# The product with v in 64 by 64 cells from a dense tile, apart from the scores

## The chip, the cores and the metric

One core of a Trainium2 chip runs the whole kernel. The metric is the device time of the program in microseconds, the median of several runs. The engines are named as the profile names them: PE is TensorE (matmuls; PEld its weight loads), DVE is VectorE, ACT is ScalarE, POOL is GpSimd, SP issues DMAs.

## The reference

Attention over chunks of 32 queries with a short window and 8 memory keys, followed by a two-layer network with a squared ReLU. Four batches, 8 heads, 768 tokens, head size 64; the network is 512 by 2048 by 512 on 3072 tokens.

```python
chunk, left_ctx, right_ctx = (32, 16, 8); n_mem = 8
for c in range(nc):                       # 24 chunks of a sequence
    k_full = concat([mem_k, k[l_start:r_end]]); v_full = concat([mem_v, v[l_start:r_end]])
    scores = scale * q_c @ k_full.T
    a = exp(scores - max(scores)); a = a / (sum(a) + 1e-09)
    out[c_start:c_end] = a @ v_full
x = out.transpose(0, 2, 1, 3).reshape(B * S, H * D)
h = x @ w_in
g = s * maximum(h, 0) ** 2 + b
return g @ w_out
```

Each chunk sees 16 + 32 + 8 context keys and 8 memory keys, a cell of 64 keys (`CELL`).

## The kernel before

Everything that the engines do is first listed as operations (`op`, line 208) with an engine, a held time from the table `HOLD` (line 134), a due time (`prio`) and the parts of tiles that they read and write. `Plan.lay` (line 229) plays that list through on a model of five engines and fixes the order of each; the program is then written out in that order. On each engine the instructions run in the order so found. An operation takes the earliest due among those that are ready; a due time is in steps, 40 for the first part and 3.75 for each of the 22 units of the second. Lists such as `VISITS`, `FLIPS`, `MIX`, `XSUM` hold due times, and `MIXENG`, `XENG`, `XENG1` choose VectorE or GpSimd for operations that either can do.

The tokens go in 8 groups of 384 (`ch`, two per batch). Attention of one group is made in two *visits* (`attend(ch, d)`), each with two pairs of heads. Groups 0 and 1 are made early. The later visits, 12 in all (groups 2 to 7), lie spread among the matmuls of the network, which fill TensorE otherwise: `hidden` (line 847) and `result` (line 870) for the groups 0 to 3, then units (`unit`, line 1041; `second`, line 1095) that make two groups of a batch together with seven products instead of eight.

A later visit goes so. `product` (line 667) makes the scores, 24 matmuls for each pair of heads, with 64 rows (the head size), 32 stationary columns (queries) and 64 moving columns (keys). VectorE and ScalarE make the softmax. `flip` (line 627) turns blocks of 32 by 32 on VectorE and sends them with eight DMAs into the tile `aT`, so that keys lie along the partitions. There two chunks of 64 keys are stacked, in a block-diagonal form: a chunk's 64 rows stand beside zeros in the columns of the other chunk. `value2` (line 684) makes the product with v from it, 24 matmuls with 128 rows, 64 stationary columns (v) and 64 moving columns (two chunks of 32 queries), into two PSUM banks, the first for 512 columns and the second for 256. All matmuls of the attention are in fp32, and each shows in the trace as two instructions with a weight load each. The network's matmuls are in the float32r form with high and low halves, which is why each result is split by ScalarE (`xhigh`, or `park` for the later groups) and VectorE (`xlow`).

For `aT` of the later visits there is one place (`diag`, line 452), the same memory that the two tiles of the early visits have. The values of a visit are made when the next visit begins: lines 786 to 795 put `value1`, `value2`, `scores1` and `scores2` in one chain, which TensorE runs without anything between, and which takes four PSUM banks (`S` and `V`, two each) at one time. Only the last visit's values stand alone (`last_[3]`, line 1198).

In `sums` (line 913) and `sums_of_parts` (line 948) sums and differences of the parked values are made, 768 columns each, and `mix` (line 982) does the like with weights.

Of the kernel before, what the change touches and what calls it, by code (L numbers as in the profile page):

```python
# [15 lines left out]
AF = mybir.ActivationFunctionType  # L16
# [61 lines left out]
POOLED = set()  # L78
MIX = [24.4, 26.07, 28.76, 31.57, 35.54, 36.93, 32.73, 30.93]
MIXENG = ['DVE', 'DVE', 'POOL', 'DVE', 'POOL', 'DVE', 'DVE', 'DVE']  # L80
XENG = ['POOL', 'POOL', 'DVE', 'POOL']
RELEASE = 22
AHEAD = -0.81
FLIPS = [3.49, 8.13, 6.86, 5.1, 9.6, 5.37, 4.05, -0.05, -0.86, 9.11, -1.0, -2.32]
PROD = [-0.08, 0.96, 0.26, 1.59, 3.42, 3.01, 3.43]
CHAIN = {'11': 1.68, '22': 0.22, '12': 4.42, '21': 6.47}
SECONDS = [6.99, 8.34, 6.63, 10.26]
XSUM = [1.29, -2.52, 0.98, -0.03]
XENG1 = ['DVE', 'POOL', 'POOL', 'POOL', 'DVE', 'DVE', 'POOL', 'DVE', 'DVE', 'POOL']
XSUM1 = [2.5, -0.8, 2.75, 1.29, 0.06, -0.47, 0.2, -3.8, 9.08, -7.14]  # L90
XSPLIT1 = [-5.65, -14.64, -0.76, -1.78]
XSPLIT = [-3.43, -3.64, 1.94, -0.12, 2.77, 4.93, 0.47]
RBANKS = 2
# [25 lines left out]
UNIT = 3.75  # L119
VISITS = [17.38, 22.0, 24.84, 30.0, 32.33, 43.05, 47.62, 56.46, 54.35, 67.42, 76.83, 76.57, 88.7]  # L120

# [6 lines left out]
for _u, (_, _f) in enumerate(STEPS):  # L128
# [4 lines left out]

HOLD = dict(hidden=523, result=690, half=365, first=850, scores=650, value1=1000, value2=530, scores1=500, scores2=600, turn=110, value=515, wrest=800, warm=215,
            relu=390, square=390, affine=565, high=388, xhigh=388, xhigh0=480, xhigh1=300, wscale=560, whigh=525, copy=270, exp6=480, exp3=340, keep=390, keepv=470, store=480,
            low=540, rec=90, edge=20, max6=490, max3=280, sub6=500, sub3=300, sum6=560, sum3=310, flip=580, xlow=470, xlow0=640, xlow1=400, wlow=350, wjoin=620, wsign=610, wdiff=610, out=600,
            small=235, part=290, wide=1040, tiny=200, norm6=1000, norm3=650, mul6=470, mul3=270, issue=440,
            prod=1036, result2=1362, save=482, hadd=554, hsq=553, hrelu=488, hsquare=517, haffine=706, hhigh=525, hlow=580,
            park0=589, park1=376, pre=1880, prev=936, khigh=840, klow=1000, accum=689, outcopy=597,
            mix2=1450, mix1=1000, mix2v=680, mix1v=410, thigh=623, tlow=675)  # L140
# [3 lines left out]
RATE, LAND, NEAR, FAR = 408.0, 2150.0, 6, 3400.0  # L144
CODE = dict(prod=12, result2=12, hidden=6, result=6, half=6, first=96, scores=96, value1=64, value2=32, scores1=96, scores2=96, turn=2, value=32)
BLOCK, SKEW = 256, 69
# [231 lines left out]
def body(ctx: ExitStack, tc: tile.TileContext, qkv, w1, w2, out):  # L378
# [72 lines left out]
    diags = Ring([wide_[:, n] for n in range(2)])  # L451
    diag = Ring([wide_])
    stats = Ring(stat_tiles)
# [185 lines left out]

    def attend(ch, d):  # L640
# [43 lines left out]
        def value2(m, V):  # L684
            for m6 in (2 * m, 2 * m + 1):
                for cp in range(2):
                    for n in range(2):
                        at = (((m6 % GB) * 2 + cp) * 2 + n) * D
                        to = V[m // 2].tile.rearrange("k (m r c q) -> k m r c q", r=2, c=2, q=CHUNK)[n * D:(n + 1) * D, m6 % 4, :, cp, :]
                        nc.tensor.matmul(to, vals_[m6 // GB].tile[:, at:at + D], aT[0].tile[:, n, :, cp * 2 * GB + m6, :], start=True, stop=True)  # L690

        def value(m, V):
# [3 lines left out]
            for c in range(NQC):  # L696
                for n in range(2):
                    half, at = divmod(((m * NQC + c) * 2 + n) * D, VW)
                    to = V[m // 2].tile.rearrange("k (m r c q) -> k m r c q", r=2, c=NQC, q=CHUNK)[n * D:(n + 1) * D, m % 2, :, c, :]
                    nc.tensor.matmul(to, vals_[half].tile[:, at:at + D], aT[n].tile[:, :, m * NQC + c, :], start=True, stop=True)  # L700

        def store(V):
            if ch >= 4:
                i = 2 * (ch % HALVES) + d
                for r in range(2):
                    lo, hi = (0, 4 * QB) if r == 0 else (4 * QB, 6 * QB)
                    firsts.append((ch // HALVES, 8, op("ACT", f"park{r}", due - 4, lambda lo=lo, hi=hi, r=r: nc.scalar.activation(park(i)[:, lo:hi], V[r].tile[:, :hi - lo], AF.Copy),
                       list(V[r].parts.values()), (c_park[i][r],))))
                if i == 3:
                    sums(ch // HALVES)  # L710
                return
            at = due + 0.9 if alone else due - 4
            for r in range(2):
                lo, hi = (0, 4 * QB) if r == 0 else (4 * QB, 6 * QB)
                to = lambda a, lo=lo, hi=hi: x.tile[:, (2 * a + d) * 2 * TOK + lo:(2 * a + d) * 2 * TOK + hi]
                fro = lambda r=r, lo=lo, hi=hi: V[r].tile[:, :hi - lo]
                got, kind = [z for z in V[r].parts.values()], str(r)
                op("ACT", "xhigh" + kind, at, lambda to=to, fro=fro: nc.scalar.activation(to(0), fro(), AF.Copy), got, (x["H", d, r],))
                op("DVE", "xlow" + kind, at, lambda to=to, fro=fro: nc.vector.tensor_tensor(to(1), fro(), to(0).bitcast(F32), ALU.subtract),
# [15 lines left out]
        def parts(V, at):  # L735
            return [op("PE", f"value{i + 1}", at, lambda ms=ms: [value(m, V) for m in ms], reads(ms), [V[i][0]]) for i, ms in enumerate(((0, 1), (2,)))]

        def soft(S):
            t, y = (None, None) if early else (Val(both), Val(diag))
            for n in range(2):  # L740
# [40 lines left out]
        else:  # L781
# [6 lines left out]
            for o in chain[1:]:  # L788
                for v in o.vals:
                    if v.ring is ps and v not in chain[0].vals:  # L790
                        chain[0].vals.append(v)
                        v.left += 1
            for o, nxt in zip(chain, chain[1:]):
                o.next = nxt
                if o not in nxt.deps:
                    nxt.deps.add(o)
            if last:
# [418 lines left out]
    for n in range(2):  # L1216
        hold(both, n, on(ts_))
    hold(diag, 0, on(diags))
    for n in range(7):
# [52 lines left out]
```

## Time and profile before

| | |
|---|---|
| median of 3 runs | 584.6 us (582.42 to 585.76) |
| profiled execution | 582.78 us, its span 581.0 us |
| TensorE busy | 571.2 us (98%) |
| VectorE, ScalarE, GpSimd busy | 381.0, 351.8, 58.0 us |
| bytes moved by DMA | 115.11 MB |

The span runs from the first to the last instruction of one profiled execution; some 2 us of the time lie around it. A line of a group gives the source line, engine, operation, output and input tiles, shape (partitions by elements; for matmuls first rows by columns of the stationary operand), the count, the busy time in us and the mean ns of one. In a timeline or a chain the first number is the start in us and the second the length.

### The profile page before, as it was taken

The numbers are of one execution on the slowest core, as the hardware profiler recorded it, in microseconds if no ns is written. First come the engines' busy times: TensorE is split into PE (matmuls) and PEld (weight loads), VectorE is DVE, ScalarE is ACT, GpSimd is POOL, SyncE is SP. The second block draws the span as 40 slices with busy tenths as digits, with TensorE's granted clock in tenths as the row PEclk, the third lists the DMA queues.
The fourth block names the chain that finished last, engine by engine and source line by source line (L and its number), as shares of the span: only waits on it lengthen the run. The fifth ranks groups of instructions, "written<-read, shape, count | busy, mean of one in ns | idle before, by whom it ended". The sixth has DMA issues, their size and how long they took to land.

```text
span 581.0 us, 12457 instructions
## 1 busy us (share of the span) xinstructions
PE 571.2 (98%) x4925; PEld 506.0 (87%) x4925; DVE 381.0 (66%) x796; ACT 351.8 (61%) x727; POOL 58.0 (10%) x59
## 2 busy tenths in 40 slices
PE   8989999999999999999999999999999999999997
PEld 4678998989889889899888899898999999999996
DVE  4988989988768988564769654565457434444442
ACT  6999888957657667454466454534466554444443
POOL 1000000001532241010131010011021000000000
PEclk9999999999999999999999999999999999999999
DMA  8995867843867978654674763745524543433002
GB/s 334 417 381 174 328 201 231 251 161 145 311 222 263 335 265 281 181 192 148 221 270 136 256 237 100 217 165 175 162 80 138 177 151 109 144 96 126 33 0 109
DMA packets 41882, 115.11 MB, mean 198 GB/s; under 512 B 5216, under 2 KB 13664, under 8 KB 41824
## 3 DMA queue, kind: packets, MB, share of 16 engines
q1 hardware_dynamic: 41824, 114.32, 57.4%
q8 instruction: 39, 0.64, 0.4%
q14 instruction: 19, 0.16, 0.1%
HBM read 88.61 MB, written 20.97 MB: 189 GB/s over the span
## 4 chain that ended last, share of the span: by engine, by line
PE 83%; DVE 6%; ACT 5%; DMA 4%; issue 1%; SPq 0%; ACTq 0%; DVEq 0%
PE ps L1053 27%; PE ps L1103 16%; PE ps L1133 16%; PE ps L879 9%; PE ps L855 9%; PE ps L690 3%; PE ps L675 3%; DMA words<-w 2%; DMA mixed<-words 1%; DMA early<-qkv 1%; ACT t L586 1%; DVE wv L837 1%; ACT ps L865 1%; DVE gL L867 1%; PE ps L700 1%
## 5 line engine op out<-in xcount | busy, mean ns | idle before, releaser
L1053 PE MATMUL ps<-x,ww 128*128 128x384 f32 x528 | 104.4, 336 | 0.0
L1072 ACT ACTIVATE gH<-words 128x384 fp32r<-128x384 f32 x66 | 34.6, 524 | 108.0 <-PE ps L1103 107.0
L1053 PEld LDWEIGHTS ps<-x,ww 128*128 128x128 f32 x528 | 93.8, 188 | 5.6
L1069 DVE TENSOR_TENSOR words<-ps,wv 128x384 f32<-128x384 f32 x66 | 34.9, 553 | 66.8 <-PE ps L1053 61.6
L1053 PE MATMUL ps<-home,ww 128*128 128x384 f32 x396 | 77.7, 338 | 0.0
L1053 PEld LDWEIGHTS ps<-home,ww 128*128 128x128 f32 x396 | 69.6, 188 | 2.9
L1150 DVE TENSOR_TENSOR partial<-ps,partial 128x512 f32<-128x512 f32 x57 | 39.2, 688 | 48.3 <-PE ps L1133 48.3
L1071 ACT ACTIVATE words<-words,b_sb,s_sb 128x384 f32<-128x384 f32 x88 | 61.7, 704 | 15.1 <-DVE words L1070 14.4
L855 PE MATMUL ps<-x,ww 128*128 128x384 f32 x288 | 54.4, 338 | 0.0
L1073 DVE TENSOR_TENSOR gL<-words,gH 128x384 fp32r<-128x384 f32 x66 | 38.5, 584 | 20.7 <-ACT gH L1072 19.5
L855 PEld LDWEIGHTS ps<-x,ww 128*128 128x128 f32 x288 | 50.4, 188 | 1.9
L600 POOL TENSOR_TENSOR t<-t,rden 128x384 f32<-128x384 f32 x24 | 20.6, 870 | 259.9 <-DVE rden L596 173.1
L1060 ACT ACTIVATE wv<-ps 128x384 f32<-128x384 f32 x66 | 31.9, 487 | 23.1 <-PE ps L1053 21.8
L1103 PE MATMUL ps<-w,gH 128*128 128x512 f32 x144 | 44.5, 390 | 0.0
L879 PE MATMUL ps<-ww,gH 128*128 128x512 f32 x144 | 44.4, 390 | 0.0
L1103 PE MATMUL ps<-ww,gH 128*128 128x512 f32 x120 | 37.1, 390 | 0.0
L855 PE MATMUL ps<-x,home 128*128 128x384 f32 x192 | 36.6, 339 | 0.0
L1070 DVE SCALAR_TENSOR_TENSOR words<-words 128x384 f32<-128x384 f32 x66 | 35.9, 549 | 0.5
L855 PEld LDWEIGHTS ps<-x,home 128*128 128x128 f32 x192 | 33.4, 188 | 1.1
L879 PEld LDWEIGHTS ps<-ww,gH 128*128 128x128 f32 x144 | 27.0, 188 | 4.9
L863 ACT ACTIVATE ps<-ps 128x384 f32<-128x384 f32 x40 | 19.2, 480 | 19.2 <-PE ps L855 18.8
L867 DVE TENSOR_TENSOR gL<-ps,gH 128x384 fp32r<-128x384 f32 x40 | 22.0, 551 | 13.1 <-ACT gH L866 13.0
(133 smaller groups left out, 1073.5 us busy)
## 6 DMA issues: line engine op xcount, KB each, us to landing
ww<-mixed SPq DMA_DIRECT2D x44, 512.0 KB, 3.8
raw<-qkv SPq DMA_DIRECT2D x28, 576.0 KB, 7.0
words<-w SPq DMA_DIRECT2D x24, 512.0 KB, 5.0
ww<-first SPq DMA_DIRECT2D x22, 512.0 KB, 4.0
v<-qkv SPq DMA_DIRECT2D x28, 384.0 KB, 4.8
mixed<-words SPq DMA_DIRECT2D x16, 512.0 KB, 3.8
out<-partial SPq DMA_DIRECT2D x23, 256.0 KB, 2.1
ww<-last SPq DMA_DIRECT2D x11, 512.0 KB, 3.4
```

Source lines behind the costliest of these rows:

```text
L855: nc.tensor.matmul(h.tile[:, :TOK], weight_tile(0, f)[:, wi, c * P:(c + 1) * P], xt(x, xi, c), start=(c == 0 and n == 0), stop=(c == NC_T ...
L879: nc.tensor.matmul(acc.tile[:, lo:hi], g.tile[gi][:, t * P:(t + 1) * P], weight_tile(1, f)[:, wi, lo:hi], start=(first and n == 0), stop=( ...
L1053: nc.tensor.matmul(bank.tile[:, :TOK], w(wi)[:, c * P:(c + 1) * P], operand(spot(b, i), xi)[:, c * TOK:(c + 1) * TOK], start=start and c = ...
L1060: op("ACT", "save", at + prio, lambda: nc.scalar.activation(v.tile, bank.tile[:, :TOK], AF.Copy), (bank[0],), (v[0],))
L1069: op("DVE", "hadd", at + prio, lambda: nc.vector.tensor_tensor(h.tile, bank.tile[:, :TOK], add.tile, ALU.add), (bank[0], add[0]), (h[0],))
L1070: op("DVE", "hsq", at + prio, lambda: nc.vector.scalar_tensor_tensor(h.tile, h.tile, 0.0, h.tile, ALU.max, ALU.mult), (), (h[0],), lock=True)
L1071: op("ACT", "haffine", at + prio, lambda: nc.scalar.activation(h.tile, h.tile, AF.Identity, scale=s_sb, bias=b_sb), (c_s[0], c_b[0]), (h[0],))
L1072: op("ACT", "hhigh", at + prio, lambda: nc.scalar.activation(g.tile[0], h.tile, AF.Copy), (h[0],), (g["H"],))
L1073: op("DVE", "hlow", at + prio, lambda: nc.vector.tensor_tensor(g.tile[1], h.tile, g.tile[0].bitcast(F32), ALU.subtract), (h[0], g["H"]), ( ...
L1103: nc.tensor.matmul(to.tile, g.tile[gi][:, t * P:(t + 1) * P], weight_tile(1, f)[:, wi, :], start=start and n == 0, stop=stop and n == 2)
L1133: nc.tensor.matmul(r.tile[:, lo:hi], gd[1, order[n]].tile[gi][:, t * P:(t + 1) * P], weight_tile(1, 2 * j + order[n])[:, wi, lo:hi], start ...
L1150: op("DVE", "accum", at + SECONDS[3], lambda r=r, o=o: nc.vector.tensor_tensor(o.tile, r.tile, o.tile, ALU.add), (r[0],), (o[0],))
```

## The change

The product with v in the later visits is made for each chunk by itself: 64 rows, 64 stationary columns, 32 moving columns, 48 matmuls per visit instead of 24. `aT` holds no zeros there and is half as large; two such tiles take the memory of the one. The upper 64 rows of the array write to the first PSUM bank and the lower to the second, 384 columns each, so that the evictions write with gaps (`spread`). Values and scores are two chains with due times of their own, the new list `VALS` for the values. The lists of due times and engines are others, and the table of held times follows the new shapes.

```diff
-MIXENG = ['DVE', 'DVE', 'POOL', 'DVE', 'POOL', 'DVE', 'DVE', 'DVE']
-XENG = ['POOL', 'POOL', 'DVE', 'POOL']
+MIXENG = ['DVE', 'DVE', 'POOL', 'DVE', 'DVE', 'DVE', 'DVE', 'DVE']
+XENG = ['DVE', 'DVE', 'POOL', 'DVE']
-AHEAD = -0.81
+AHEAD = -1.44
+VALS = [0.94, 4.58, 1.7, 1.28, 1.6, -0.5, 0.26, 3.17, 6.28, 4.28, 1.39, 5.89]
-XENG1 = ['DVE', 'POOL', 'POOL', 'POOL', 'DVE', 'DVE', 'POOL', 'DVE', 'DVE', 'POOL']
+XENG1 = ['POOL', 'POOL', 'POOL', 'POOL', 'DVE', 'DVE', 'POOL', 'DVE', 'DVE', 'DVE']
-VISITS = [17.38, 22.0, 24.84, 30.0, 32.33, 43.05, 47.62, 56.46, 54.35, 67.42, 76.83, 76.57, 88.7]
+VISITS = [16.16, 20.44, 24.84, 31.33, 34.66, 40.42, 47.25, 58.08, 56.92, 70.56, 73.87, 79.75, 85.65]
...
-HOLD = dict(hidden=523, result=690, half=365, first=850, scores=650, value1=1000, value2=530, scores1=500, scores2=600, turn=110, value=515, wrest=800, warm=215,
+HOLD = dict(hidden=523, result=690, half=365, first=850, scores=650, value1=620, value2=330, scores1=500, scores2=600, turn=110, value=515, wrest=800, warm=215,
...
-    diag = Ring([wide_])
+    cells = Ring([wide_[:, n] for n in range(2)])
...
-                    aT.tile[row:row + CHUNK, :, c // 2, c % 2 * 2 * GB:(c % 2 + 1) * 2 * GB, :].rearrange("k n m q -> k n (m q)"),
-                    t.tile[c * CHUNK:(c + 1) * CHUNK, :, g * w:(g + 1) * w]), [*made_, c_diag[0], c_diag[1]], (aT[c, g],), size=CHUNK * 2 * w * 4)
+                    aT.tile[row:row + CHUNK, :, c % 2 * 2 * GB:(c % 2 + 1) * 2 * GB, :].rearrange("k n m q -> k n (m q)"),
+                    t.tile[c * CHUNK:(c + 1) * CHUNK, :, g * w:(g + 1) * w]), made_, (aT[c, g],), size=CHUNK * 2 * w * 4)
...
-                    for n in range(2):
-                        at = (((m6 % GB) * 2 + cp) * 2 + n) * D
-                        to = V[m // 2].tile.rearrange("k (m r c q) -> k m r c q", r=2, c=2, q=CHUNK)[n * D:(n + 1) * D, m6 % 4, :, cp, :]
-                        nc.tensor.matmul(to, vals_[m6 // GB].tile[:, at:at + D], aT[0].tile[:, n, :, cp * 2 * GB + m6, :], start=True, stop=True)
+                    for r in range(2):
+                        for n in range(2):
+                            at = (((m6 % GB) * 2 + cp) * 2 + n) * D
+                            rows, col = slice(r * CELL, (r + 1) * CELL), (2 * m6 + cp) * CHUNK
+                            nc.tensor.matmul(V[r].tile[n * D:(n + 1) * D, col:col + CHUNK], vals_[m6 // GB].tile[rows, at:at + D],
+                                             aT[0].tile[rows, n, cp * 2 * GB + m6, :], start=True, stop=True)
...
+        spread = lambda x, r: x.rearrange("k (m r z) -> k r m z", r=2, z=2 * CHUNK)[:, r]
+        dense = lambda v: v.tile[:, :TOK].rearrange("k (m z) -> k m z", z=2 * CHUNK)
...
-                    lo, hi = (0, 4 * QB) if r == 0 else (4 * QB, 6 * QB)
-                    firsts.append((ch // HALVES, 8, op("ACT", f"park{r}", due - 4, lambda lo=lo, hi=hi, r=r: nc.scalar.activation(park(i)[:, lo:hi], V[r].tile[:, :hi - lo], AF.Copy),
+                    firsts.append((ch // HALVES, 8, op("ACT", "park", due - 4, lambda r=r: nc.scalar.activation(spread(park(i), r), dense(V[r]), AF.Copy),
...
-            return [op("PE", f"value{i + 1}", at, lambda ms=ms: [value(m, V) for m in ms], reads(ms), [V[i][0]]) for i, ms in enumerate(((0, 1), (2,)))]
+            return [op("PE", f"value{i + 1}", at, lambda ms=ms: [value(m, V) for m in ms], reads(ms), [V[0][i], V[1][i]]) for i, ms in enumerate(((0, 1), (2,)))]
...
-            chain = last[0](V, a - 0.05) if last else []
-            chain += [op("PE", f"scores{p + 1}", a - 0.05, lambda p=p: product(p, S, p), (raws_[p][0],), (S[0][p], S[1][p])) for p in pairs]
...
+            chains = [[op("PE", f"scores{p + 1}", a - 0.05, lambda p=p: product(p, S, p), (raws_[p][0],), (S[0][p], S[1][p])) for p in pairs]]
+            if last:
+                chains.append(last[0](V, a - VALS[2 * (ch - NALONE) + d]))
+            for chain in chains:
...
```

## Rows read from the trace of the kernel before

**Rows 1.** The page's first table: engine, busy us, share of span, instructions.

```profile
PE 571.2 (98%) x4925; PEld 506.0 (87%) x4925; DVE 381.0 (66%) x796; ACT 351.8 (61%) x727; POOL 58.0 (10%) x59
```

**Rows 2.** The page's 40 slices: the granted TensorE clock in tenths.

```profile
PEclk9999999999999999999999999999999999999999
```

**Rows 3.** The chain that ended last, 121 to 132 us: start, length, work.

```profile
122.43 2.15 PE ps L879 x9
124.58 1.55 PE ps L690 x48
126.13 1.12 PE ps L675 x73
127.26 2.29 PE ps L855 x12
```

**Rows 4.** Waits of TensorE: total us, times, longest.

```profile
PE ps L879 <- DVE gL L867: 1.5, 5, 0.7
PEld ps L879 <- DVE gL L867: 3.6, 7, 1.1
```

**Rows 5.** Line 690's instructions: ns min/median/max, first and last start, shape.

```profile
L690 PEld LDWEIGHTS ps<-aT,v x576: 132/138/138, 124.5 to 428.1; 128*64 128x64 f32 x192
L690 PE MATMUL ps<-aT,v x576: 222/222/271, 124.5 to 428.1; 128*64 128x64 f32 x192
```

**Rows 6.** Timeline of the weight loads, 124 to 127.5 us.

```profile
124.51 1.48 PEld L690 LDWEIGHTS ps<-aT,v 128*64 128x64 f32 x48 [0.35 <-issue]
```

**Rows 7.** Line 675 alone by stretch: length, PE busy (instructions), PEld busy, clock.

```profile
126.06:127.19 1.13, 1.13 (x96) 1.03 (x96) 1.00 0.63 134
126.06:126.31 0.25, 0.25 (x32) 0.25 (x33) 1.00 0.29 66
```

**Rows 8.** Line 675's matmuls, as rows 5.

```profile
L675 PE MATMUL ps<-raw x1344: 212/216/241, 21.6 to 395.7; 64*32 64x64 f32 x192
```

**Rows 9.** Line 855's matmuls, as rows 5.

```profile
L855 PE MATMUL ps<-x,ww x288: 335/336/445, 82.1 to 210.6; 128*128 128x384 f32 x144
```

**Rows 10.** Timeline of TensorE, 424.5 to 429.6 us, the last visit's values.

```profile
424.57 1.21 PE L1053 MATMUL ps<-x,ww 128*128 128x384 f32 x6
425.61 1.21 PE L1053 MATMUL ps<-home,ww 128*128 128x384 f32 x6
426.75 1.62 PE L690 MATMUL ps<-aT,v 128*64 128x64 f32 x48
428.29 1.31 PE L1053 MATMUL ps<-home,ww 128*128 128x384 f32 x6
429.44 0.40 PE L1103 MATMUL ps<-ww,gL 128*128 128x512 f32 x1
```

**Rows 11.** DMA issues: count, KB each, us to landing.

```profile
aT<-t SPq DMA_DIRECT2D x96, 48.0 KB, 2.0
```

**Rows 12.** ScalarE's groups by shape, line 707: busy us, mean ns.

```profile
L707 ACT ACTIVATE park<-ps 128x512 f32<-128x512 f32 x8 | 4.8, 595 | 3.8 <-PE ps L690 3.8
L707 ACT ACTIVATE park<-ps 128x256 f32<-128x256 f32 x8 | 3.0, 381 | 0.0
```

**Rows 13.** VectorE's and GpSimd's groups by shape, as rows 12.

```profile
L1002 DVE TENSOR_TENSOR words<-words 128x256 f32<-128x256 f32 x6 | 4.1, 691 | 0.0
L999 DVE TENSOR_TENSOR words<-words 128x512 f32<-128x512 f32 x6 | 4.1, 684 | 0.0
...
L918 DVE TENSOR_TENSOR park<-words,park 128x768 f32<-128x768 f32 x2 | 1.9, 950 | 0.0
...
L918 POOL TENSOR_TENSOR park<-park 128x768 f32<-128x768 f32 x4 | 7.4, 1856 | 10.3 <-DVE park L918 10.1
```

**Rows 14.** Busy us by stretch: length, PE, PEld, DVE, ACT, POOL, clock, DMA share, GB/s.

```profile
165.00:190.00 25.00, 25.00 (x257) 22.59 (x257) 18.88 (x38) 15.75 (x31) 9.49 (x9) 1.00 0.72 256
190.00:216.00 26.00, 25.59 (x258) 22.52 (x257) 24.00 (x43) 16.89 (x34) 8.92 (x6) 1.00 0.87 302
```

**Rows 15.** The page's DMA queues: packets, MB, share of 16 engines.

```profile
q8 instruction: 39, 0.64, 0.4%
```

More of the change, by code (lines that the diff above doesn't have):

```diff
@@ L78 @@
 POOLED = set()
-MIX = [24.4, 26.07, 28.76, 31.57, 35.54, 36.93, 32.73, 30.93]
-MIXENG = ['DVE', 'DVE', 'POOL', 'DVE', 'POOL', 'DVE', 'DVE', 'DVE']
-XENG = ['POOL', 'POOL', 'DVE', 'POOL']
+MIX = [26.6, 21.97, 27.08, 33.84, 34.32, 32.59, 34.4, 29.48]
+MIXENG = ['DVE', 'DVE', 'POOL', 'DVE', 'DVE', 'DVE', 'DVE', 'DVE']
+XENG = ['DVE', 'DVE', 'POOL', 'DVE']
 RELEASE = 22
-AHEAD = -0.81
[L84 to L88, printed above, removed]
-XENG1 = ['DVE', 'POOL', 'POOL', 'POOL', 'DVE', 'DVE', 'POOL', 'DVE', 'DVE', 'POOL']
-XSUM1 = [2.5, -0.8, 2.75, 1.29, 0.06, -0.47, 0.2, -3.8, 9.08, -7.14]
-XSPLIT1 = [-5.65, -14.64, -0.76, -1.78]
-XSPLIT = [-3.43, -3.64, 1.94, -0.12, 2.77, 4.93, 0.47]
+AHEAD = -1.44
+VALS = [0.94, 4.58, 1.7, 1.28, 1.6, -0.5, 0.26, 3.17, 6.28, 4.28, 1.39, 5.89]
+FLIPS = [3.01, 10.26, 7.96, 6.04, 12.49, 10.24, 4.67, -0.19, -2.81, 9.31, 1.66, -3.48]
+PROD = [-0.02, -0.36, 0.64, 3.0, 4.82, 3.15, 2.04]
+CHAIN = {'11': 2.25, '22': -1.34, '12': 3.8, '21': 9.85}
+SECONDS = [8.25, 9.05, 8.73, 6.92]
+XSUM = [4.44, 5.03, 2.66, 0.05]
+XENG1 = ['POOL', 'POOL', 'POOL', 'POOL', 'DVE', 'DVE', 'POOL', 'DVE', 'DVE', 'DVE']
+XSUM1 = [3.04, -4.96, -1.23, 1.1, -0.21, -0.67, 2.18, -2.39, 9.32, -5.02]
+XSPLIT1 = [-2.16, -12.11, -0.26, -1.27]
+XSPLIT = [-3.33, 2.91, -3.28, -0.55, 1.56, 7.3, -1.34]
 RBANKS = 2
@@ L131 @@
 LATE_F = NF - NEARLY
[L134 to L136 removed]
+HOLD = dict(hidden=523, result=690, half=365, first=850, scores=650, value1=620, value2=330, scores1=500, scores2=600, turn=110, value=515, wrest=800, warm=215,
+            relu=390, square=390, affine=565, high=388, xhigh=388, xhighh=400, xhigh0=480, xhigh1=300, wscale=560, whigh=525, copy=270, exp6=480, exp3=340, keep=390, keepv=470, store=480,
+            low=540, rec=90, edge=20, max6=490, max3=280, sub6=500, sub3=300, sum6=560, sum3=310, flip=580, xlow=470, xlowh=530, xlow0=640, xlow1=400, wlow=350, wjoin=620, wsign=610, wdiff=610, out=600,
             small=235, part=290, wide=1040, tiny=200, norm6=1000, norm3=650, mul6=470, mul3=270, issue=440,
             prod=1036, result2=1362, save=482, hadd=554, hsq=553, hrelu=488, hsquare=517, haffine=706, hhigh=525, hlow=580,
[L139 removed]
+            park=480, pre=1880, prev=936, khigh=840, klow=1000, accum=689, outcopy=597,
             mix2=1450, mix1=1000, mix2v=680, mix1v=410, thigh=623, tlow=675)
@@ L144 @@
 RATE, LAND, NEAR, FAR = 408.0, 2150.0, 6, 3400.0
-CODE = dict(prod=12, result2=12, hidden=6, result=6, half=6, first=96, scores=96, value1=64, value2=32, scores1=96, scores2=96, turn=2, value=32)
+CODE = dict(prod=12, result2=12, hidden=6, result=6, half=6, first=96, scores=96, value1=128, value2=64, scores1=96, scores2=96, turn=2, value=32)
 BLOCK, SKEW = 256, 69
@@ L717, in store @@
                 got, kind = [z for z in V[r].parts.values()], str(r)
+                if not early:
+                    to = lambda a, r=r: spread(x.tile[:, (2 * a + d) * 2 * TOK:(2 * a + d + 1) * 2 * TOK], r)
+                    fro, kind = lambda r=r: dense(V[r]), "h"
                 op("ACT", "xhigh" + kind, at, lambda to=to, fro=fro: nc.scalar.activation(to(0), fro(), AF.Copy), got, (x["H", d, r],))
@@ L735, in parts @@
         def parts(V, at):
-            return [op("PE", f"value{i + 1}", at, lambda ms=ms: [value(m, V) for m in ms], reads(ms), [V[i][0]]) for i, ms in enumerate(((0, 1), (2,)))]
+            return [op("PE", f"value{i + 1}", at, lambda ms=ms: [value(m, V) for m in ms], reads(ms), [V[0][i], V[1][i]]) for i, ms in enumerate(((0, 1), (2,)))]
         def soft(S):
-            t, y = (None, None) if early else (Val(both), Val(diag))
+            t, y = (None, None) if early else (Val(both), Val(cells))
             for n in range(2):
@@ L785, in attend @@
             V = [Val(ps, "V") for _ in range(2)] if last else []
-            chain = last[0](V, a - 0.05) if last else []
-            chain += [op("PE", f"scores{p + 1}", a - 0.05, lambda p=p: product(p, S, p), (raws_[p][0],), (S[0][p], S[1][p])) for p in pairs]
[L788 to L796, printed above, removed]
+            chains = [[op("PE", f"scores{p + 1}", a - 0.05, lambda p=p: product(p, S, p), (raws_[p][0],), (S[0][p], S[1][p])) for p in pairs]]
+            if last:
+                chains.append(last[0](V, a - VALS[2 * (ch - NALONE) + d]))
+            for chain in chains:
+                for o in chain[1:]:
+                    for v in o.vals:
+                        if v.ring is ps and v not in chain[0].vals:
+                            chain[0].vals.append(v)
+                            v.left += 1
+                for o, nxt in zip(chain, chain[1:]):
+                    o.next = nxt
+                    if o not in nxt.deps:
+                        nxt.deps.add(o)
             if last:
@@ L1217, in body @@
         hold(both, n, on(ts_))
-    hold(diag, 0, on(diags))
+    for n in range(2):
+        hold(cells, n, on(diags))
     for n in range(7):
```

## The prediction

> **What bounds the kernel now.** I read the page's first table before anything else: TensorE is busy for 571 of 581 us, VectorE for two thirds of the span, ScalarE for less [rows 1]. The slices beneath it show the clock granted in full in all 40 of them, the 2.4 GHz level [rows 2], so clock is no term here. A busy TensorE could still be one that waits inside its instructions, so the chain of waits comes next. Around the first later visit it is TensorE alone: matmuls of the hidden layer, 48 value instructions in 1.55 us, the scores, hidden layer again, with nothing of another engine between [rows 3]. The waits of TensorE on other engines sum to a few microseconds in the whole span, the largest being on VectorE's low halves [rows 4]. So the time is the length of TensorE's instruction stream, and the change is worth what it does to that stream's length. From 430 us on no visit is left and nothing changes.
>
> **What a visit costs now.** There are 576 value instructions, 48 in each of 12 visits (24 products in fp32, two passes each) [rows 5]. A block takes 1.55 us to the next block [rows 3]. The weight loads of a block run for 1.48 us in all, one of them for 138 ns [rows 5, 6]: the last begins 1.34 us after the first, 23 steps later, so a pair (one load and matmul in each half of the columns) takes 58 ns; 24 pairs are 1.40 us, and 0.15 us is the emptying of the array before another shape starts. The scores have 96 instructions in 1.13 us, 32 of them seen in the first 0.25 us [rows 7].
>
> What holds a pair at 58 ns decides this case. The first matmul of a block waits for its own weights, and that shows as its longest duration less the median: 49 ns for 64 columns, 25 for 32, 109 for 128 [rows 5, 8, 9]. So a load costs about 0.8 ns a column, 25 ns or so per 32 columns, whether it fills 64 rows (scores) or 128. A 64-column load is then 49 to 55 ns. The matmul over 64 moving fp32 columns is about as long: the scores run their 32 first matmuls as four sets of eight in 0.25 us, some 56 to 62 ns a set, with loads of half the length. Load and matmul overlap in a tile (49 + 56 would exceed 58), and a set lasts as long as the longer one plus a few ns.
>
> **The change part by part.**
> *The products.* 48 products instead of 24 per visit, 96 instructions instead of 48, now in four tiles (two halves of the rows, two of the columns) rather than two. So there are 24 sets as before. In each the matmul has half the columns (about 27 ns), but each tile still loads 64 weight columns, 49 to 55 ns. No row shows 64 by 64 tiles, so I bound a set from both sides. From above: the load sets it, 58 ns as now, block 1.55 us. From below: the load hides, the set halves to 29 ns, block 0.70 + 0.15 = 0.85 us. Between lies the pace at which instructions come: the scores, also 96 instructions with 96 loads, need 1.13 us though their first 32 were quick, and their loads are half as long. I take 1.55: the nearest row for a 64-column load is the present block, and the scores show that fewer rows don't shorten a load. Saving: nothing, ends 0 and 0.70 us a visit.
>
> The Trainium skill, TensorEngine Tiling (Array Packing), Theoretical Speedup, gives up to 2x for a contraction of at most 64; by that the block would be 0.85 us, the lower end above. The same page, Instruction Overhead, speaks against the change: it says a matmul with one moving column has the latency of one with 60, and that no tiling factor should be taken from a dimension that is already small; by that the 32 columns would cost what 64 do and the block would stay at 1.55. No row here has 32 moving columns, so neither is shown.
>
> *Apart from the scores.* Each block now has its own entry and exit. The last visit of before shows a value block alone: six hidden-layer matmuls take 1.04 us, the six ahead of the block 1.14, the six behind it 1.15 [rows 10]. So entry costs 0.10 and exit 0.11 us. Today values and scores share them in 11 visits; apart, each of the 11 pays 0.21 more: +2.3 us, all on the path. Two that fall side by side would save their 0.21; I take all 11.
>
> *Dense tile, two buffers.* The same eight transfers of 48 KB per visit to places of the same size [rows 11]; SP's queue gets no more of them. The tile of the next visit no longer waits until the last one was read: worth at most the waits of TensorE that exist, and none is on this tile; 0.
>
> *Evictions.* Halves of 512 and 256 columns become two of 384. ScalarE now takes 595 + 381 ns [rows 12]; by columns two of about 490. Both wait for the whole block instead of one for two thirds of it: the first starts up to 0.5 us later, with ScalarE's later work behind it, which idles over a third of the span [rows 1]. 0; without that cover 0.5 us for 12 visits, 6 us, which I don't expect since TensorE has other work between a visit and its sums.
>
> *Moves between VectorE and GpSimd, new due times.* One mix goes from GpSimd to VectorE: three operations of 0.68 us and three of half their size at up to 0.69 us [rows 13], at most 4.1 us of VectorE time; I take 3.7, somewhere between 140 and 216 us. Three additions of the parked values in the later batches go over too, 0.95 us where GpSimd takes 1.86 [rows 13], and one goes back; there VectorE has room. In the last stretch ahead of the units VectorE is busy for 24.0 of 26 us and TensorE already loses 0.41 [rows 14]. A longer TensorE stream gives these waits room: I take back 0.4 us, ends -1.5 (every wait on low halves in the span) and +1.5 (as much again).
>
> *More instructions.* 1152 more for TensorE, at 0.64 MB for 9850 [rows 1, 15] some 75 KB, or five more fetches in addition to 39. No wait on a fetch shows near a visit; 0.
>
> **Sum.** 0 + 2.3 - 0.4 = +1.9 us. Against the profiled execution (582.78 us, span 581.0) that is 584.7; the median of the runs is 584.6, 1.8 higher, and the change adds the same there: 586.5. With the ends of the waits +0.8 to +3.8 us, 585.4 to 588.4.
>
> **The rivals.**
> *Instruction pace decides (0.19).* The load hides, and the block takes what the scores take, 1.13 us: 11 x (1.13 - 1.55 + 0.21) - 0.42 = -2.7 us, 581.9. For it: the scores have the same count of instructions and four to eight tiles at work. The planner's table in the diff goes further, 950 ns for a block where it had 1530; that is a number of the code and no row. Against: the scores' loads are half as wide.
> *The set halves (0.08).* Block 0.85 us: 11 x (0.85 - 1.55 + 0.21) - 0.70 = -6.1 us, 578.5. Against: 96 instructions in 0.70 us is faster than the scores ever are over such a length. The speedup rule of the tiling page is this case.
> *VectorE becomes the bound ahead of the units (0.11), the slower side.* If over 2.0 us of the moved mix falls within 190 to 216 us, its busy time exceeds the stretch [rows 14], and low halves come late to TensorE. With all of the 3.7 us there the overflow is 1.7 us, and 3.7 us if the idle time is no use to it; with the 2.3 us of entries and exits +4.0 to +6.0, say 589.6. Against: the due times moved as well, and the mix can lie earlier, where VectorE idles for a quarter of the time [rows 14].
> *Loads of the two halves of the rows take turns (0.02).* A set is then 116 ns: 12 x 1.38 + 2.3 = +18.9 us, 603.5. Against: no score matmul waits longer than 241 - 216 = 25 ns for its weights [rows 8], one load, though its neighbour in the other rows loads at the same time.
>
> **How the numbers follow.** The likeliest, 0.60, is the load-bound set: 586.5. The range takes in the instruction pace and most of the VectorE case: 581.0 to 589.6. About 0.5%, 2.9 us, is what a measurement can tell from no change. Faster than 581.7: the halved set and somewhat over half of the pace case, 0.20. Slower than 587.5: VectorE, the turns, and the upper part of the forecast (0.07), 0.20. Same: 0.60.
>
> **What would show it.** The value line in the profile after: 1152 instructions; one block 1.5 us long (right), 1.1 (pace), below 0.9 (halved). Six hidden-layer matmuls behind each value block and behind each scores block in 1.15 us rather than 1.04. TensorE's busy time up by about 2 us. If the stretch ahead of the units shows TensorE waiting on low halves for more than 2 us in all, VectorE it was. The forecast falls if the block is clearly under 1.3 us.

## The result and the profile after

The changed kernel takes 587.84 us (median of 20 runs) where the kernel before takes 584.22 us in the same session: 1.0065 of it, 95% interval 1.0045 to 1.0084, so 3.6 us slower. The profiled execution went from 582.78 to 586.53 us, its span from 581.0 to 584.7. The forecast was +1.9 us, 586.5, within 581.0 to 589.6.

From the page of the kernel after, the busy times and the queue of instructions (answering to [rows 1, 15]):

```profile
PE 573.4 (98%) x5501; PEld 506.4 (87%) x5501; DVE 389.4 (67%) x806; ACT 352.1 (60%) x727; POOL 46.1 (8%) x49
...
q8 instruction: 43, 0.70, 0.5%
```

Its waits of TensorE, grouped by the pair of lines: total us, number, longest (as [rows 4]):

```profile
PEld ps L889 <- DVE gL L877: 4.3, 3, 2.8
PE ps L889 <- DVE gL L877: 3.2, 2, 2.5
```

TensorE is as busy as before, 98%, only longer, and one wait on VectorE's low halves is 2.5 us where none was above 0.7. The value matmuls (line 692 now) by line, as [rows 5]:

```profile
L692 PEld LDWEIGHTS ps<-aT,v x1152: 129/135/136, 96.8 to 409.2; 64*64 64x64 f32 x192
```

And the last value block in the timeline of TensorE: start, duration, operation, as [rows 10]:

```profile
407.83 1.60 PE L692 MATMUL ps<-aT,v 64*64 64x32 f32 x96
409.36 0.50 PE L1113 MATMUL ps<-ww,gL 128*128 128x512 f32 x1
409.69 0.63 PE L1113 MATMUL ps<-ww,gH 128*128 128x512 f32 x2
410.16 0.40 PE L1113 MATMUL ps<-ww,gL 128*128 128x512 f32 x1
410.39 0.62 PE L1113 MATMUL ps<-ww,gH 128*128 128x512 f32 x2
```

Twice the instructions, each with half the moving columns, and the block takes 1.53 us to the next start, where it took 1.54 to 1.55. So do nine of the twelve blocks; the other three, at 97, 145 and 221 us, take 1.65, 1.83 and 2.49 us, with gaps between their instructions. The weight load is as long as it was (135 ns, 138 before). The first matmul behind the block needs 0.33 us to the next, a like one later 0.23: the exit. A scores block has its own now, entry and exit, in the same timeline:

```profile
117.18 2.25 PE L865 MATMUL ps<-x,ww 128*128 128x384 f32 x12
119.36 1.20 PE L676 MATMUL ps<-raw 64*32 64x64 f32 x96
120.49 0.50 PE L889 MATMUL ps<-ww,gL 128*128 128x512 f32 x1
120.82 0.63 PE L889 MATMUL ps<-ww,gH 128*128 128x512 f32 x2
```

Twelve hidden-layer matmuls take 2.18 us to the scores where a dozen takes 2.08: entry 0.10. The block itself is unchanged, 1.13 us.

And the stretch ahead of the units, first the timeline of TensorE:

```profile
190.42 2.25 PE L865 MATMUL ps<-x,ww 128*128 128x384 f32 x12
195.12 0.50 PE L889 MATMUL ps<-ww,gL 128*128 128x512 f32 x1 [2.45 <-DVE gL L877]
```

That of VectorE:

```profile
186.28 1.98 DVE L1010 TENSOR_TENSOR words<-words 128x256 f32<-128x256 f32 x1
188.18 2.06 DVE L1012 TENSOR_TENSOR words<-words 128x256 f32<-128x256 f32 x1
190.17 2.07 DVE L1011 TENSOR_TENSOR words<-words 128x256 f32<-128x256 f32 x1
```

That of GpSimd:

```profile
183.82 4.16 POOL L971 TENSOR_TENSOR park<-x 128x768 f32<-128x768 f32 x2 [7.63 <-ACT x L726]
188.05 1.91 POOL L971 TENSOR_TENSOR park<-park 128x768 f32<-128x768 f32 x1
190.04 1.92 POOL L971 TENSOR_TENSOR park<-park,x 128x768 f32<-128x768 f32 x1
```

Three small operations of a mix on VectorE (lines 1010 to 1012) take 2.0 us each, where the same lines take 0.41 elsewhere, as long as an addition on GpSimd beside them. The low half that TensorE waits for is behind them, by way of ScalarE. Its timeline:

```profile
192.27 1.15 ACT L1018 ACTIVATE words<-words 128x512 fp32r<-128x512 f32 x2 [4.07 <-DVE words L1011]
193.33 0.62 ACT L875 ACTIVATE ps<-ps,b_sb,s_sb 128x384 f32<-128x384 f32 x1
193.98 0.49 ACT L876 ACTIVATE gH<-ps 128x384 fp32r<-128x384 f32 x1
```

ScalarE's next instruction in its fixed order (line 1018) needs the result of the mix and waits 4.07 us for it; its work on the hidden layer (lines 875 and 876) stands behind that, and VectorE's low half (line 877) needs line 876. The busy time of each engine by stretch, as [rows 14]:

```profile
190.00:216.00 26.00, 23.55 (x122) 21.53 (x121) 24.06 (x45) 17.97 (x36) 4.41 (x3) 1.00 0.60 212
```

VectorE is busy for 24.06 us there, before 24.00; TensorE loses 2.45 us, before 0.41.

Where the 3.7 us of the two spans are, worked out from the starts of all matmuls in both traces: each gap is put down to what stands before and behind it, with the usual spacing (174 ns for 384 columns, 227 for 512) taken off.

| part of TensorE's time, us | before | after | difference |
|---|---|---|---|
| entries and exits of value and scores blocks | 6.35 | 8.40 | +2.05 |
| inside the 12 value blocks | 16.76 | 17.14 | +0.38 |
| waits of over 0.14 us on other engines from 60 us on | 1.44 | 2.61 | +1.17 |
| one hole within a block | 0.64 | 0.83 | +0.19 |
| the rest (small gaps, start, end) | | | -0.05 |

The 0.38 us inside the blocks lie in the blocks at 97 and 145 us, whose first instructions come up to 0.11 us apart. From its first start to its last a block without gaps takes 1.38 us, before 1.40.

### The profile page after: what moved, and what is told of

It reads as the page before. It is cut to its first block, busy times and chain, and to the rows that moved or that the text cites. A ratio compares the mean times of both kernels' runs of the same rounds, so it can differ in the third digit from the quotient of the medians.

```text
span 584.7 us, 13595 instructions
## 1 busy us (share of the span) xinstructions
PE 573.4 (98%) x5501; PEld 506.4 (87%) x5501; DVE 389.4 (67%) x806; ACT 352.1 (60%) x727; POOL 46.1 (8%) x49
## 4 chain that ended last, share of the span: by engine, by line
PE 92%; DVE 3%; ACT 3%; DMA 1%; issue 1%; SPq 0%; ACTq 0%
PE ps L1063 28%; PE ps L1113 16%; PE ps L1143 15%; PE ps L889 13%; PE ps L865 13%; PE ps L692 3%; PE ps L676 2%; ACT t L587 1%; DMA early<-qkv 1%; PE ps L703 1%; DVE words L1011 0%; DVE words L1012 0%; DVE wv L847 0%; DVE words L1010 0%; DVE x L727 0%
## 5 line engine op out<-in xcount | busy, mean ns | idle before, releaser
L1083 DVE TENSOR_TENSOR gL<-words,gH 128x384 fp32r<-128x384 f32 x66 | 36.9, 568 | 86.9 <-ACT gH L1082 86.7
L1063 PE MATMUL ps<-home,ww 128*128 128x384 f32 x396 | 79.6, 337 | 0.0
L1081 ACT ACTIVATE words<-words,b_sb,s_sb 128x384 f32<-128x384 f32 x88 | 60.3, 703 | 19.5 <-DVE words L1080 19.1
L889 PE MATMUL ps<-ww,gH 128*128 128x512 f32 x144 | 44.5, 390 | 0.0
L1113 PE MATMUL ps<-w,gH 128*128 128x512 f32 x108 | 33.3, 390 | 0.0
L1143 PE MATMUL ps<-w,gH 128*128 128x512 f32 x108 | 33.3, 390 | 0.0
L889 PE MATMUL ps<-ww,gL 128*128 128x512 f32 x72 | 29.0, 402 | 2.5 <-DVE gL L877 2.5
```

The source lines that it names most:

```text
L889: nc.tensor.matmul(acc.tile[:, lo:hi], g.tile[gi][:, t * P:(t + 1) * P], weight_tile(1, f)[:, wi, lo:hi], start=(first and n == 0), stop=( ...
L1063: nc.tensor.matmul(bank.tile[:, :TOK], w(wi)[:, c * P:(c + 1) * P], operand(spot(b, i), xi)[:, c * TOK:(c + 1) * TOK], start=start and c = ...
L1081: op("ACT", "haffine", at + prio, lambda: nc.scalar.activation(h.tile, h.tile, AF.Identity, scale=s_sb, bias=b_sb), (c_s[0], c_b[0]), (h[0],))
L1083: op("DVE", "hlow", at + prio, lambda: nc.vector.tensor_tensor(g.tile[1], h.tile, g.tile[0].bitcast(F32), ALU.subtract), (h[0], g["H"]), ( ...
L1113: nc.tensor.matmul(to.tile, g.tile[gi][:, t * P:(t + 1) * P], weight_tile(1, f)[:, wi, :], start=start and n == 0, stop=stop and n == 2)
L1143: nc.tensor.matmul(r.tile[:, lo:hi], gd[1, order[n]].tile[gi][:, t * P:(t + 1) * P], weight_tile(1, 2 * j + order[n])[:, wi, lo:hi], start ...
```

## The experiments

My theory after the result: the value block did not shrink because each tile still loads 64 columns of weights; 2.05 us are the entries and exits; and the rest is VectorE, stretched by GpSimd at 184 to 192 us. Rivals: the moving columns or the instructions set the block; being apart is free and all of the loss is VectorE; VectorE simply has too much to do.

### What sets the value block

Twice the moving columns, plan unchanged:

```diff
+ k = min(cp * 2 * GB + m6, 4 * GB - 2)
- ...(V[r].tile[n * D:(n + 1) * D, col:col + CHUNK], vals[rows, at:at + D], aT[0].tile[rows, n, cp * 2 * GB + m6, :])
+ ...(V[r].tile[n * D:(n + 1) * D, col:col + 2 * CHUNK], vals[rows, at:at + D], aT[0].tile[rows, n, k:k + 2, :])
```

> The changed kernel, its plan unchanged, with 64 moving columns in each value matmul instead of 32 (two neighbouring query blocks; the product is not the reference's). Theory, the 64-column weight load sets the pace of a value block: a set of four tiles stays at 58 ns, a block at 1.4 to 1.55 us, the time at 1.006 of before, as the changed kernel. Rival, the moving columns set it: a set grows by some 27 ns, a block by 0.64 us, the time by 7.7 us to 1.02 of before.

Half the stationary columns with twice the moving ones, the shape of the scores:

```diff
+ to, at, col = n * D + cp * CHUNK, at + cp * CHUNK, 2 * m6 * CHUNK
+ ...(V[r].tile[to:to + CHUNK, col:col + 2 * CHUNK], vals[rows, at:at + CHUNK], aT[0].tile[rows, n, m6:m6 + 2, :])
```

> The changed kernel, its plan unchanged, with 32 stationary columns instead of 64 and 64 moving columns instead of 32 in each value matmul; still 48 per visit, now of the very shape of the scores (cells are mixed up, the product is not the reference's). Theory, the weight load sets the pace: the loads halve and a block takes what the scores take, 1.13 us instead of about 1.5, so 12 x 0.35 = 4.2 us less than the changed kernel, near 0.999 of before. Rival, the moving columns or the number of instructions set it: the block stays at 1.5 us or grows, 1.006 of before or more.

Measured: 1.0080 (1.0055 to 1.0104) for the wide one, 1.0018 (1.0000 to 1.0035) for the narrow one. Their timelines of TensorE at the first value block, first the wide, then the narrow:

```profile
96.41 1.63 PE L693 MATMUL ps<-aT,v 64*64 64x64 f32 x96
97.97 0.50 PE L890 MATMUL ps<-w,gL 128*128 128x512 f32 x1
```

```profile
96.97 1.30 PE L693 MATMUL ps<-aT,v 64*32 64x64 f32 x96
98.20 0.50 PE L890 MATMUL ps<-w,gL 128*128 128x512 f32 x1
```

1.56 us with 64 moving columns, 1.23 with 32 stationary ones. Inside the 12 blocks the sums, with the longest holes taken out, are 17.20 and 13.24 us against 17.14 of the changed kernel. What sets them shows in the starts of the matmuls. A set here is one matmul in each tile of the array: two tiles before, four in the changed and the wide kernel, eight in the narrow one. In blocks without holes, from the start of a set to that of the next:

| kernel | stationary, moving columns | first set to second, ns | later sets, ns |
|---|---|---|---|
| before | 64, 64 | 107 | 58 |
| changed | 64, 32 | 80 | 58 |
| wide | 64, 64 | 107 | 58 |
| narrow | 32, 64 | 80 | 56 (second to fourth) |

The first step reads as a stream and a load one after the other: 32 moving columns less take 27 ns off, and so do 32 loaded ones, so by these differences 64 columns of either take some 53 ns. Later the two overlap. With 64 loaded columns the sets stay 58 ns apart whether 32 or 64 columns move, so the moving columns don't set the pace; and the narrow block has 96 instructions too, so their number doesn't hold it at 1.53 us either. What is left is the load, the longer of the two in the changed kernel.

The narrow kernel supports this less than it seems: its block isn't shorter because a set is (56 ns with 64 moving columns), but because a set holds eight matmuls instead of four. After the first 32 its matmuls come some 13 ns apart. No run has a short load and a short stream in four tiles, so that a shorter load alone would shorten the changed block is argued and not shown. Its block was expected at 1.13 us and its time at 0.999; both came out longer. Its profiled execution has holes and, behind the wait at 192 us, a granted clock of 0.50 from 195 to 198 us.

### Joined again, and apart alone

Values and scores in one chain, the rest of the change kept (planned anew):

```diff
-            chains = [[op("PE", f"scores{p + 1}", ...) for p in pairs]]
-            if last:
-                chains.append(last[0](V, a - VALS[2 * (ch - NALONE) + d]))
+            chains = [last[0](V, a - 0.05) if last else []]
+            chains[0] += [op("PE", f"scores{p + 1}", ...) for p in pairs]
```

> The changed kernel with values and scores in one chain again, due with the scores; cells, the two tiles and all other due times as in the change, and the order of all engines is planned anew. Theory, the separate entries and exits cost 0.2 us in each of 11 visits: TensorE's stream is 2.1 us shorter in those, and with the 1.2 us more of waits on VectorE left as they are the time is 1.003 of before. Rival, all of the loss is the wait on VectorE ahead of the units: the time stays at 1.006 if that wait stays over 2 us, and goes to 1.000 if it goes.

Measured: 1.0324 (1.0293 to 1.0356). Neither theory had this. Its waits of TensorE:

```profile
PE ps L676 <- issue: 7.8, 4, 2.4
```

And its timeline of TensorE at one visit:

```profile
143.13 1.60 PE L692 MATMUL ps<-aT,v 64*64 64x32 f32 x96
144.67 0.82 PE L676 MATMUL ps<-raw 64*32 64x64 f32 x60
147.01 0.62 PE L676 MATMUL ps<-raw 64*32 64x64 f32 x36 [1.52 <-issue]
```

In the middle of the scores TensorE stands for 1.5 us with nothing that the profile shows to wait for; four such holes make 7.8 us, and stretches at a lower clock follow the longest (0.59 from 204 to 208 us, 0.50 from 321 to 324). The separate entries are gone as expected. So I asked whether the instructions come too late: 96 + 96 pairs of load and matmul are 384 instructions at once, before the change 288. The same kernel and plan with 24 value matmuls of 64 moving columns (half of the products left out):

> The kernel with values and scores joined, its plan unchanged, but with 24 value matmuls of 64 rows, 64 stationary and 64 moving columns per visit (half of the products left out, the rest over two query blocks). Theory, the holes of 1.7 to 2.6 us within the scores of the joined kernel come from instructions that arrive too late, since 384 instructions follow at once: with 288, as before the change, the holes within blocks fall from 8.9 us to 1 us or less in all. Rival, they come from data or from the shape of the tiles: they stay.

Measured: 1.0051 (1.0026 to 1.0076). No hole is left within a block: "issue" is gone from the waits on the scores (TensorE's time in such holes 8.9 us in the joined kernel, 0 here). Other waits on VectorE came instead, as the plan was not made for it. So the holes of the joined kernel go with the value instructions that were left out. But one chain isn't needed for holes: in the profiled executions of the wide and the narrow kernel a scores block by itself, at 149 us and 2.3 us behind the end of a value block, has one too, of 1.26 and 0.90 us, both behind its 79th instruction.

That TensorE waits for the fetch of its instructions shows in the times of the packets of 16 KB in queue q8 (43 after, 39 before), worked out from the traces. With each hole named "issue" within a block, the last packet before the hole's end:

| kernel | hole's end, us | packet, us | from the packet's end to the hole's, us |
|---|---|---|---|
| before, scores | 331.64 | 329.23 to 330.16 | 1.48 |
| changed, values | 223.01 | 220.57 to 221.45 | 1.56 |
| joined, scores above | 147.01 | 144.70 to 145.61 | 1.40 |
| wide, scores | 150.83 | 147.16 to 149.41 | 1.42 |
| narrow, scores | 150.58 | 147.24 to 149.64 | 0.94 |

The joined kernel's other holes end 1.22 to 1.42 us behind a packet. Holes within blocks that the profile puts down to a transfer or to VectorE (in the runs with the chains of before apart and with true held times, below) end 4.9 us or more behind the last packet. So these holes are instructions that come late. That many short ones within a few microseconds make them late fits the half variant; how far each fetch runs ahead was not tested.

The other way round, the kernel before with only the chains taken apart:

```diff
-            chain = last[0](V, a - 0.05) if last else []
-            chain += [op("PE", f"scores{p + 1}", ...) for p in pairs]
+            chains = [[op("PE", f"scores{p + 1}", ...) for p in pairs]]
+            if last:
+                chains.append(last[0](V, a - 1.0))
```

> The kernel before with one part of the change alone: values and scores as two chains, the values due one step ahead of the scores; matmuls, tile, due times and engines as before, planned anew. Theory: 11 more entries and exits of 0.2 us, +2.2 us, 1.004 of before, with at most 1 us either way from waits. Rival, being apart costs nothing: 1.000, and no longer gaps of the first matmuls behind the blocks.

Measured: 1.0160 (1.0130 to 1.0190), 9.3 us more. Some 2 us are the entries and exits; most of the rest is one place, where the scores wait for their load (timeline of TensorE):

```profile
226.16 0.97 PE L675 MATMUL ps<-raw 64*32 64x64 f32 x48 [2.89 <-DMA raw<-qkv]
227.60 0.97 PE L675 MATMUL ps<-raw 64*32 64x64 f32 x48 [0.47 <-DMA raw<-qkv]
228.50 2.29 PE L1055 MATMUL ps<-x,ww 128*128 128x384 f32 x6
```

Six matmuls then take 2.29 us, where they take 1.04 otherwise: the granted clock is 0.50 from 228 to 233 us. The due times were not made for two chains, so as a price of being apart this run is inconclusive; the price stands on the rows of the changed kernel, and no run isolates it.

### The wait ahead of the units

The five additions on GpSimd issued on VectorE, in the same place of an unchanged plan:

```diff
- lambda e: e.tensor_tensor(park(to), a(), c(), o)
+ lambda e: nc.vector.tensor_tensor(park(to), a(), c(), o)
```

> The changed kernel, its plan unchanged, with the five additions of the last stretch ahead of the units that run on GpSimd issued on VectorE in the same place of the order (0.95 us each). Theory, GpSimd's additions beside VectorE's mix stretch the mix (0.41 to 2.0 us an operation) and this makes TensorE wait 2.6 us at 192 us: the three operations fall back to 0.42 us, VectorE does the additions in less than it lost, the wait falls under 1 us and the time by 1.5 us or more, to 1.004 of before or less. Rival, VectorE simply has too much to do there: with 4.75 us more on it the wait grows, and the time is over 1.0065.

Measured: 1.0007 (0.9987 to 1.0026), median 584.63 us. VectorE's timeline at the same mix:

```profile
187.55 0.55 DVE L877 TENSOR_TENSOR gL<-ps,gH 128x384 fp32r<-128x384 f32 x1
188.02 0.68 DVE L1009 TENSOR_TENSOR words<-words 128x512 f32<-128x512 f32 x1
188.73 0.42 DVE L1010 TENSOR_TENSOR words<-words 128x256 f32<-128x256 f32 x1
189.08 0.42 DVE L1012 TENSOR_TENSOR words<-words 128x256 f32<-128x256 f32 x1
189.41 0.42 DVE L1011 TENSOR_TENSOR words<-words 128x256 f32<-128x256 f32 x1
```

And the busy time of each engine in the stretch from 190 to 216 us:

```profile
190.00:216.00 26.00, 25.97 (x191) 23.36 (x179) 23.97 (x46) 18.82 (x38) 2.43 (x2) 1.00 0.71 241
```

The operations are back at 0.42 us, TensorE loses 0.03 us of these 26, and VectorE, with the additions on it, is busy no longer than before. So VectorE had room; it was held up. The transfers are not what held it: the DMA engines are as busy from 184 to 192 us in both (0.94 and 0.93). By the runs most of the loss goes with this one edit.

The profiled execution doesn't show that gain. At 586.63 us it is the longest of the 12, and its span, 584.9 us, is that of the changed kernel (584.7). Two holes take the place of the wait: one of 0.7 us in the value block at 222 us, as in the changed kernel, and one in a scores block by itself (timeline of TensorE):

```profile
149.85 1.02 PE L676 MATMUL ps<-raw 64*32 64x64 f32 x79
152.41 0.35 PE L676 MATMUL ps<-raw 64*32 64x64 f32 x17 [1.54 <-issue]
```

TensorE's instructions and their order are the same in both kernels, and the changed kernel's profiled execution has no hole in this block. The packet of instructions ahead of it ran from 148.15 to 150.99 us here, 2.84 us where 0.97 is the median, and the hole ends 1.42 us behind it; in the changed kernel's execution it took 1.16 us (146.90 to 148.06). So such a hole comes in some executions and not in others.

Was it the plan's short held times for the value block that brought them side by side?

```diff
-value1=620, value2=330
+value1=1000, value2=530
```

> The changed kernel planned with the value block's held times of the kernel before (1000 and 530 ns, as it measures) instead of 620 and 330. Theory, GpSimd and VectorE collide at 184 to 192 us because the plan takes TensorE to be 0.55 us a visit faster than it is, so that their shares of the work lie elsewhere than planned: with true times the wait of 2.6 us falls under 1 us and the time goes to 1.004 of before or less. Rival, the due times were fitted to the short blocks, or the collision has nothing to do with them: the wait stays over 2 us or others come, 1.0065 or more.

Measured: 1.0095 (1.0068 to 1.0122). The theory falls: the additions lie beside the same mix (1.98, 2.06 and 2.07 us) and the wait stays, in its waits of TensorE:

```profile
PE ps L889 <- DVE gL L877: 3.9, 4, 2.5
```

With true held times and all ten sums planned on VectorE:

> As the kernel with the true held times, and the ten sums of parts ahead of the units planned on VectorE alone. Theory, with both causes of the collision gone TensorE's waits on low halves are those of before (1.4 us) or less, and what is left is the 2.1 us of entries and exits: 1.003 to 1.004 of before. Rival, VectorE is full there: a wait of over 2 us remains, 1.0065 or more. Below 1.000 would beat both kernels; neither theory expects it.

Measured: 1.0049 (1.0026 to 1.0072). The mix is short again, but the new order has a wait of 2.0 us on a transfer into `aT` and 1.8 us on a low half at a scores block, and its profiled execution, 591.38 us, is the longest of its 12; so this tells little of the entries.

Last, the same move of the additions in the kernel before:

> The kernel before, its plan unchanged, with the five additions ahead of the units that run on GpSimd issued on VectorE in the same place of the order. Theory, GpSimd's additions stretch two operations of a mix in the kernel before too (0.41 to 1.1 and 2.07 us near 206 us), which gives its wait of 0.4 us at 211 us: up to 0.8 us less, 0.999 to 1.000 of before, so that the changed kernel with the same move stays slower by its entries and exits, about 2 us less what the plan gives back. Rival, VectorE has no room for 4.75 us more there in this order: a new wait of 1 us or more and 1.002 or above.

Measured: 0.9997 (0.9979 to 1.0016): no change, so in the kernel before the two stretched operations cost nothing that shows. None of these kernels is shown to be faster than the kernel before.

## Why the prediction was right

The time, 587.84 us, lies within the forecast range and 1.3 us above its likeliest value; as a difference the runs have +3.6 us where the sum has +1.9. The main mechanism, an unchanged block with entries and exits on top, came as forecast. That the rest stayed within the range is in part luck: its upper end was set for a rival whose place came true and whose mechanism did not.

**The block (0 us, right).** Forecast 1.55 us by the load-bound set, measured 1.53 in nine blocks and 1.65 to 2.49 in the three with gaps; the sums inside the blocks grew by 0.38 us. The step that carried it, the first matmul's excess over the median as the length of a load (49 ns for 64 columns), is borne out by the steps from first to second set (some 53 ns). Both rivals with a shorter block fall: the instruction pace needs 1.13 us, the halved set 0.85. The rival of loads that take turns falls with them: later sets are 58 ns apart, not 116.

Of the two rules of the Trainium skill, TensorEngine Tiling (Array Packing), the one under Theoretical Speedup does not show here: 64 contracted rows gave no time back. The one under Instruction Overhead gives the outcome, an unchanged block, but not the reason: 32 moving columns did take less than 64 here (27 ns off the first step), and it is the sets behind it that stay at 58 ns with either.

**Entries and exits (+2.3, right).** Measured +2.05, all 11 visits: 0.10 into a scores block, 0.11 out of a value block. This is read from the starts in two traces, and no experiment confirmed it by time.

**What the waits give back (-0.4, wrong sign).** Measured +1.17 in the profiled execution. The prediction did have this place and its bound: the ends of the waits were -1.5 and +1.5, and a rival named low halves late ahead of the units. By the prediction's own sign, over 2 us of such waits in the stretch, it was VectorE: 2.45 us. But its mechanism was VectorE's load, with the moved mix in 190 to 216 us. That mix ran at 167 to 171 us, in three operations of 0.69 and three of 0.42 us, and harmed nothing; VectorE's busy time in the stretch is the same. What failed is that I counted GpSimd's work as off the path and priced its moves by their own length; the sum names the moves of `MIXENG` and `XENG` and none of `XENG1`, whose additions are the ones that ran beside the mix. A row of before had shown it: in its timeline at 207 us one of these operations takes 2.07 us beside an addition on GpSimd.

```profile
206.84 1.91 POOL L961 TENSOR_TENSOR park<-park,x 128x768 f32<-128x768 f32 x1
206.97 2.07 DVE L1002 TENSOR_TENSOR words<-words 128x256 f32<-128x256 f32 x1
208.96 0.41 DVE L1001 TENSOR_TENSOR words<-words 128x256 f32<-128x256 f32 x1
```

That is also where the 691 ns mean of [rows 13] for half the columns came from, which I took for a plain duration. The Trainium skill, SBUF — State Buffer (SBUF: two separate sides), says that VectorE, in operations with two SBUF inputs among others, and GpSimd share a pair of ports under an exclusive lock, held for a whole instruction, so that the other blocks. The trace agrees: 2.0 us beside additions of 1.9.

**The clock (no term, wrong).** The profiled execution shows full clock throughout, as I assumed. But of the 20 runs 13 have a mean granted clock of 0.997 or less, with a median of 589.0 us against 586.5 for the other seven; of the 68 runs of the kernel before that were taken with the experiments, four have. In the profiled execution of the wide variant the same wait is followed by a stretch at a lower clock (by stretch, the clock is the third figure from the right):

```profile
194.00:196.00 2.00, 0.05 (x1) 0.05 (x1) 1.86 (x5) 1.97 (x5) 0.00 (x0) 1.00 0.15 60
196.00:200.00 4.00, 4.00 (x12) 3.29 (x13) 4.00 (x10) 2.85 (x6) 2.49 (x2) 0.60 0.35 142
```

So in that execution the wait of 2.5 us costs a second time: TensorE stood from 193.5 to 195.95 us, and the granted clock of the next 4 us is 0.60, the 1.2 GHz level for most of them. That the same happened in the 13 runs is argued from their mean clock; none of them was profiled. With the additions on VectorE none of 12 runs is below 0.999, which fits, and would explain why taking the wait away gave back more than its 1.2 us.

**More instructions (0, too low).** I priced 1152 more instructions at nothing, as no wait on a fetch showed near a visit. One did show: a row of before has such a hole, in the waits of TensorE, within the scores block at 330 us, and it ends 1.48 us behind a packet of instructions:

```profile
PE ps L675 <- issue: 0.5, 1, 0.5
```

In the changed kernel's profiled execution the term is small, +0.19 us for the hole. (The slow starts of two value blocks, the 0.38 us, are 4 us or more behind a packet, and their cause isn't shown.) Other executions with values and scores apart have holes of up to 1.54 us, and in one chain they reach 2.4 us. So being apart keeps twice the instructions from costing as much as they do in one chain, and the prediction costed it as if it were a choice.

**Evictions and the dense tile (0 and 0, right).** An eviction of parked values takes 488 ns on average, about the 490 forecast, and no wait of TensorE on one is listed; the waits of weight loads on the new tile are 0.2 us in all.

**What stays open.** With the wait gone the runs are at 1.0007, and the interval ends at 1.0026, or 1.5 us, where 2.05 us of entries and exits alone would give 1.0035; the medians of that session, 584.63 and 583.36 us, lie 1.3 us apart. The profiled execution can't settle it: from 60 us on its waits on other engines are 1.0 us against 1.44 before, but it has the two holes, one of them behind a slow fetch. Whether entries and exits cost less than read, or something else gives back, I can't say.

## What to carry to other kernels

Before splitting a matmul into smaller tiles, ask which of load and stream sets its pace: the excess of a block's first matmul over the median gives the load, and here cutting rows and moving columns was worth nothing while the stationary columns stayed. Count the entries into another tile shape, and how many short instructions follow within a few microseconds. When work moves to or from GpSimd, look for VectorE operations that are as long as a GpSimd instruction beside them, and who waits behind, on a third engine too. One profiled execution can be the longest of its kernel: set it beside all runs before reading a gain from it.

## What the runs showed of the hardware that was not expected

- Holes of 1.5 to 2.4 us with 192 pairs of load and matmul at once; with 96 at once, 2.3 us behind another 96, holes of 0.90 to 1.54 us in three executions and none in a fourth; with 144, 0.5 us idle in the kernel before and none in the half variant. They end 0.94 to 1.59 us behind a packet of 16 KB of instructions, which took 0.88 to 2.84 us.
- A VectorE operation of 0.41 us took 1.98 to 2.07 us beside additions on GpSimd of 1.9 us, three times in a row.
- After the same wait of 2.5 us TensorE's granted clock fell to half in the profiled executions of the wide and the narrow kernel, and not in that of the changed one.
- With 64 stationary columns a set of four 64 by 64 tiles takes 58 ns with 32 or with 64 moving fp32 columns; with 32 stationary and 64 moving columns a set of eight tiles takes 56 ns.
